# Second mixing of a fused attention kernel: eight chunks of 56 keys in place of four of 112

## The chip, the cores and the metric

The kernel runs on one core of a Trainium2 chip. The metric is device time in microseconds (us) from the first to the last instruction of one launch, with what lies around it; lower is better. Engines are called as the profile calls them: PE is TensorE (PEld its weight loads, which have rows of their own), DVE is VectorE, ACT is ScalarE, POOL is GpSimd, SP is SyncE, which issues the DMAs.

## The reference

Attention whose heads are mixed twice by small matrices, over the scores and over the probabilities, and behind it a feed-forward layer. Shapes: 4 batches, 12 heads, 448 queries and keys, head size 64; 768 and 2048 features in the feed-forward.

```
scores = scale * q @ k^T                       # per batch and head
scores = einsum('bhij,hg->bgij', scores, w_pre)     # first mixing
attn   = exp(scores - max) / (sum + 1e-9)
attn   = einsum('bhij,hg->bgij', attn, w_post)      # second mixing
x      = (attn @ v), heads side by side        # 1792 x 768
h      = x @ w_in
out    = (h * sigmoid(1.702 * h)) @ w_out
```

## The kernel before

**Steps.** The attention is cut into 180 steps, 45 for each batch, of 10 queries (8 in a batch's last one). The scores of a block of queries go to DRAM, and a step reads back a tile `r` whose partitions are (query, head) pairs: two halves of 5 queries x 12 heads = 60 partitions each, at partitions 0 and 64. `mix` and `mix_two` (the first mixing) multiply it by a small block matrix (`wa`, `wq`) into the PSUM tile `mx`; `mix_two` does two steps at once on four tiles of 64 rows x 64 columns of PE. `peak` (DVE), `expo` (ACT), `shifted` (POOL) and `inverse` (DVE) make the unnormalised probabilities `e` and the inverse sums; `weigh_mix` (POOL) makes `wr`, the second mixing's block matrix with the inverse sums in it.

**The second mixing.** `post` (line 368) is the step that the change touches. Its products have `e` as the stationary operand (what is loaded into PE: 60 rows x 112 keys) and `wr` as the moving one (60 rows x 60 columns), both float32. The result is the mixed probabilities, transposed: keys on partitions, (head, query) along the free dimension. There are 4 chunks of 112 keys and 2 row halves, so 8 products a step; the row halves run on two tiles of 64 rows x 128 columns and write to two PSUM banks of the tile `pp`, of which there is one. In the profile each float32 product stands as two weight loads and two streams, so a step has 16 of each on line 377. Then `keep_whole` (ACT, batches 0 and 1, float32) or `keep_upper` and `keep_lower` (ACT and DVE, batches 2 and 3, a float16 pair) copy `pp` into `p`, and after 12 steps `context` (lines 419 and 430) multiplies `p` with `v`, 112 keys on the partitions in each of four products.

**The feed-forward.** `hidden` (line 589) and `project` (line 628) run products of 128x128 float16 weights with 448 columns in groups of 6. They are laid between the steps as soon as a batch's `x` is ready, and go on alone after the last step. The feed-forward weights are fetched, split into float16 pairs and stored back to DRAM during the first steps (`conversion`).

**What sets the order.** A planner inside the kernel (`run_all`) puts every piece of work, with an estimated duration, on a queue of its engine and emits the instructions in that order; the engines then run their queues in order and wait on semaphores. Its table `MODE` groups the PE work by the shape of PE's tiles, and it adds 0.1 us where two neighbours differ:

```
MODE = {"qk": 1, "pp": 1, "mx": 2, "av": 3}
if MODE.get(last) != MODE.get(j["kind"]):
    occ, at = occ + 0.1, at + 0.1
```

For `post` it reckons with 0.44 us, in both kernels. Where it sees PE idle for 0.5 us or more ahead of a product, `fill` (line 287) puts float32 products of a constant with itself there, 128x128x128, on the PSUM bank that the product is about to write; they keep PE active and compute nothing that is used.

Of the kernel before, what the change touches and what calls it, by code (L numbers as in the profile page):

```python
# [10 lines left out]
F16 = mybir.dt.float16  # L11
# [8 lines left out]
B, H, S, D = 4, 12, 448, 64  # L20
# [13 lines left out]
HI = GI // 2  # L34
GAP = 64
NPAIR = H // 2
NR, CP = 4, S // 4
NCC = DM // 128
NS = 8
SW = DFF // NS  # L40
# [5 lines left out]
def attention_then_feed_forward(ctx, tc, q, k, v, w_pre, w_post, w_in, w_out, out):  # L46
    nc = tc.nc
    ctx.enter_context(tc.manual_schedule())

    def pool(name, bufs=1, **kw):  # L50
        return ctx.enter_context(tc.tile_pool(name=name, bufs=bufs, **kw))

    keep, stat, flow = pool("keep"), pool("stat", 4), pool("flow")
# [4 lines left out]
    st = {}  # L58
# [69 lines left out]


    THIRDS = 3  # L130
    SH = {"q": [128, NPAIR // THIRDS, S], "k": [128, NPAIR // THIRDS, S], "v": [CP, H // THIRDS, NR * D]}
    SRC = {"q": q, "k": k, "v": v}

    def load(name, b, i, use, tag="op"):

        t = st[name, b, i] = flow.tile(SH[name], F32, name=f"{name}{use}{i}_{b}", tag=tag, bufs=THIRDS)
        w = t.shape[1]
        nc.sync.dma_start(out=t, in_=SRC[name][b][:, i * w:(i + 1) * w])

    def load_whole(name, b, i):  # L140

        t = st[name, b, i] = flow.tile(SH[name], F32, name=f"{name}f{i}_{b}", tag=f"{name}p{i}")
        w = t.shape[1]
# [43 lines left out]
    def pair_of(name, b, i):  # L187

        key = (name + "p", b, i)
        if key not in st:  # L190
            if name == "v":
                st[key] = flow.tile([CP, 2, H // THIRDS, NR * D], F16, name=f"vp{i}_{b}", tag=f"vp{i}")
            else:
                st[key] = flow.tile([128, 2, NPAIR // THIRDS, S], F16, name=f"{name}p{i}_{b}", tag=f"{name}p{i}")
        t = st[name, b, i]
        src = t.rearrange("p a b -> p (a b)")
        u, l = (st[key][:, x].rearrange("p a b -> p (a b)") for x in range(2))
        return u, l, src, st["s" + name, b][:t.shape[0], 0:1]

    def upper_part(name, b, i, eng):  # L200
        u, _, src, s = pair_of(name, b, i)
        if eng == "A":
            nc.scalar.activation(u, src, AF.Copy, scale=s)
        elif eng == "D":
            nc.vector.tensor_scalar(u, src, s, 1.0, op0=ALU.mult, op1=ALU.mult)
        else:
            nc.gpsimd.tensor_scalar(u, src, s, 1.0, op0=ALU.mult, op1=ALU.mult)

    def lower_part(name, b, i, eng="D"):
        u, l, src, s = pair_of(name, b, i)  # L210
        nc.vector.scalar_tensor_tensor(l, src, s, u, op0=ALU.mult, op1=ALU.subtract)


    def chunk(b, c):
        i0 = c * CI
        return i0, min(CI, S - i0)
# [9 lines left out]
    def bank(name, tag="gen", bufs=NBK):  # L226
        return ps.tile([128, 512], F32, name=name, tag=tag, bufs=bufs)
# [43 lines left out]
    def rows_of(g):  # L271
        return g * GI, min(GI, S - g * GI)
# [14 lines left out]
    def fill(t):  # L287
        if gap[0] >= 0.5:
            for _ in range(int((gap[0] - 0.25) / 0.213)):
                nc.tensor.matmul(t[:, :128], ones, ones, start=True, stop=True)  # L290
        gap[0] = 0.0
# [76 lines left out]
    def post(i):  # L368
        n = rows_of(steps[i][1])[1] // 2
        w = n * H  # L370
        e, wr = row.pop(("e", i)), row.pop(("wr", i))
        pp = ps.tile([128, 2, 512], F32, name=f"pp_{i}", tag="pp", bufs=1)
        fill(pp[:, 0])
        for jc in range(NR):
            for a in range(2):
                rs = slice(a * GAP, a * GAP + w)
                nc.tensor.matmul(  # L377
                    pp[:CP, a, jc * w:(jc + 1) * w], e[rs, jc * CP:(jc + 1) * CP], wr[rs, :, :n],
                    start=True, stop=True,
                )  # L380
        row["pp", i] = pp[:CP, :, :NR * w].rearrange("p a (x i) -> p x a i", i=n)

    def mixed_to(i):
# [23 lines left out]
    def context(b, c, pr):  # L407
        i0, n = chunk(b, c)
        if pr % 3 == 0:
            av = bank(f"av_{b}_{c}_{pr}")  # L410
            fill(av)
            st["av"] = av[:, :3 * n].rearrange("p (a i) -> p a i", i=n)
        av = st["av"]
        w = H // THIRDS
        if not AV16[b]:
            for jc in range(NR):
                for d in range(2):
                    h = 2 * pr + d
                    nc.tensor.matmul(  # L419
                        av[d * D:(d + 1) * D, pr % 3, :],  # L420
                        st["v", b, h // w][:, h % w, jc * D:(jc + 1) * D],
                        st["p", b, c][:, jc, h, :n],
                        start=(jc == 0), stop=(jc == NR - 1),
                    )
            return av
        terms = [(jc, i, j) for jc in range(NR) for i, j in ((0, 0), (0, 1), (1, 0))]
        for t, (jc, i, j) in enumerate(terms):
            for d in range(2):
                h = 2 * pr + d
                nc.tensor.matmul(  # L430
                    av[d * D:(d + 1) * D, pr % 3, :],
                    st["vp", b, h // w][:, i, h % w, jc * D:(jc + 1) * D],
                    st["p", b, c][:, j, jc, h, :n],
                    start=(t == 0), stop=(t == len(terms) - 1),
                )
        return av
# [165 lines left out]
    def tanh(u, fc):  # L602
        th = st["th", u, fc] = flow.tile([128, S], F32, name=f"th_{u}_{fc}", tag="th", bufs=2)
        nc.scalar.activation(th, st["h", u, fc], AF.Tanh, scale=st["ct", u][:, 0:1])  # L604

    def gated(u, fc):
        th = st["th", u, fc]
        nc.vector.scalar_tensor_tensor(th, th, 1.0, st["h", u, fc], op0=ALU.add, op1=ALU.mult)  # L608
# [62 lines left out]
    USES = {"r": 15, "near": 10}  # L671
    MARGIN = {"in": 1.5, "w64": 1.5, "wt": 1.0}
    CROSS, SAME, LOOK = 0.12, 0.04, 0.1
    MODE = {"qk": 1, "pp": 1, "mx": 2, "av": 3}

    def add(eng, occ, f, after=(), due=0.0, lat=None, size=0.0, takes=(), kind="", bias=0.0, behind=None, moves=""):

        occ = occ if isinstance(occ, dict) else {e: occ for e in eng.split("/")}
        if lat is None:
            lat = {e: o + (0.2 if e == "PE" else 0.1) for e, o in occ.items()}  # L680
        lat = lat if isinstance(lat, dict) else {e: lat for e in occ}
        j = {"eng": tuple(occ), "occ": occ, "lat": lat, "f": f, "due": due, "size": size, "takes": list(takes),
             "kind": kind, "moves": moves, "bias": bias, "left": 0, "then": [], "next": [], "at": None, "from": 0.0}
        for a in after:
            if a is not None:
                a["then"].append(j)
                j["left"] += 1
        if behind is not None:
            behind["next"].append(j)
            j["left"] += 1  # L690
        for x in j["takes"]:
            x[1].append(j)
        if not j["left"]:
            waiting.append(j)
        return j
# [44 lines left out]
    def run_all():  # L740

        last = ""
        while waiting:
            picks = []
            for e in list(free) + ["-"]:
# [15 lines left out]
                if best:  # L761
                    t = min(x[0] for x in best) + LOOK
                    picks.append(min((x for x in best if x[0] <= t), key=lambda x: (x[2]["due"] - (2.0 if e == "PE" and last in MODE and x[2]["kind"] in MODE else 0.0), x[0]))[1:] + (e,))
            assert picks, [(j["eng"], j["due"], [x[0] for x in j["takes"]]) for j in waiting][:20]
# [4 lines left out]
            if e == "PE":  # L769
                if MODE.get(last) != MODE.get(j["kind"]):  # L770
                    occ, at = occ + 0.1, at + 0.1
# [364 lines left out]
    for i in range(N):  # L1136
        if i + AHEAD < N:
            b, g = steps[i + AHEAD]
            n = i + AHEAD
# [25 lines left out]
        b, g = steps[i]  # L1165
# [20 lines left out]
    for u in range(NU):  # L1186
        s, b = units[u]
# [6 lines left out]
        for fc in range(SF):  # L1194
# [12 lines left out]
            a = add("A", 0.53, lambda u=u, fc=fc: tanh(u, fc), [j, ct], due + 0.2, 0.64, takes=[("th", th)])  # L1207
            d = add("D", 0.54, lambda u=u, fc=fc: gated(u, fc), [a], due + 0.3, 0.62)
# [43 lines left out]
def _layout(inputs):  # L1252

    a = {n: np.asarray(inputs[n]) for n in _INS}
    for n in ("q", "k"):
        a[n] = a[n].reshape(B, NPAIR, 2, S, D).transpose(0, 2, 4, 1, 3).reshape(B, 128, NPAIR, S)
    a["v"] = a["v"].reshape(B, H, NR, CP, D).transpose(0, 3, 1, 2, 4).reshape(B, CP, H, NR * D)
    a["w_post_t"] = a["w_post"]
    w = a["moe_w_in"].reshape(NCC, 128, NS, SW).transpose(2, 1, 0, 3)
    a["moe_w_in"] = np.ascontiguousarray(w).reshape(NS, 128, WN)  # L1260
    w = a["moe_w_out"].reshape(NS, SF, 128, DM).transpose(0, 2, 1, 3)
    a["moe_w_out"] = np.ascontiguousarray(w).reshape(NS, 128, WN)
    return {n: np.ascontiguousarray(a[n]) for n in _INS}
# [20 lines left out]
```

## Time and profile before

| what | us |
|---|---|
| median of 3 runs | 929.02 (928.87 to 931.21) |
| the profiled execution | 927.6 |
| its span, first to last instruction | 925.9 |
| PE busy | 901.5 |
| ACT busy | 562.6 |
| DVE busy | 542.5 |
| mean granted TensorE clock | 0.996 of full speed |

The time of the profiled execution is 1.7 us more than its span, and 1.4 us less than the median. The first step's second mixing begins at 21.1 us and the last one's ends at about 781 us; what follows is feed-forward alone. In rows of matmuls and weight loads, `60*112` is the part of PE's array in use (rows x columns), and `60x60` is the operand (partitions x elements).

### The profile page before, as it was taken

The numbers are of one execution on the slowest core, as the hardware profiler recorded it, in microseconds if no ns is written. First come the engines' busy times: TensorE is split into PE (matmuls) and PEld (weight loads), VectorE is DVE, ScalarE is ACT, GpSimd is POOL, SyncE is SP. The second block draws the span as 40 slices with busy tenths as digits, with TensorE's granted clock in tenths as the row PEclk, the third lists the DMA queues.
The fourth block names the chain that finished last, engine by engine and source line by source line (L and its number), as shares of the span: only waits on it lengthen the run. The fifth ranks groups of instructions, "written<-read, shape, count | busy, mean of one in ns | idle before, by whom it ended". The sixth has DMA issues, their size and how long they took to land.

```text
span 925.9 us, 22628 instructions
## 1 busy us (share of the span) xinstructions
PE 901.5 (97%) x8708; PEld 548.3 (59%) x8708; DVE 542.5 (59%) x1254; ACT 562.6 (61%) x1280; POOL 264.6 (29%) x518
## 2 busy tenths in 40 slices
PE   8998998999999999989999999999999999999998
PEld 4676676556565665655656555555656555555554
DVE  4656665876768977975456755457544553333233
ACT  4867776887678697854576565555555453323442
POOL 1312332332223513351116322332123332203332
PEclk9999999999999999999999999999999999999999
DMA  6878888889878998776677585466544322344322
GB/s 218 279 234 264 268 292 267 301 297 286 301 250 284 293 319 273 254 242 212 208 249 225 159 263 164 142 206 214 174 142 125 126 95 69 123 142 137 137 70 93
DMA packets 68270, 194.42 MB, mean 210 GB/s; under 512 B 10419, under 2 KB 35123, under 8 KB 68163
## 3 DMA queue, kind: packets, MB, share of 16 engines
q1 hardware_dynamic: 68163, 192.98, 63.9%
q8 instruction: 69, 1.13, 0.5%
q14 instruction: 38, 0.31, 0.1%
HBM read 136.32 MB, written 54.04 MB: 206 GB/s over the span
## 4 chain that ended last, share of the span: by engine, by line
PE 89%; DVE 5%; ACT 2%; DMA 2%; issue 1%; POOL 0%; SPq 0%; ACTq 0%; DVEq 0%; POOLq 0%
PE h L589 23%; PE po L628 23%; PE pp L377 16%; PE mx L333 7%; PE av L419 4%; PE qk L239 3%; PE av L430 3%; PE pp L290 3%; PE qk L249 3%; PE mx L319 1%; DMA qf<-in_q_dram 1%; ACT p L396 1%; DVE w_f L518 1%; DVE nm L338 1%; DVE w_p L557 1%
## 5 line engine op out<-in xcount | busy, mean ns | idle before, releaser
L589 PE MATMUL h<-x,wt 128*128 128x448 f16 x1152 | 244.2, 353 | 0.0
L628 PE MATMUL po<-g,wt 128*128 128x448 f16 x1152 | 241.4, 353 | 0.1
L377 PEld LDWEIGHTS pp<-wr,e 60*112 60x112 f32 (+1 forms) x2880 | 158.3, 175 | 62.9 <-issue 40.0
L377 PE MATMUL pp<-wr,e 60*112 60x60 f32 (+1 forms) x2880 | 177.8, 262 | 0.0
L628 PEld LDWEIGHTS <-wt 128*128 128x128 f16 x1152 | 108.9, 98 | 113.6 <-issue 17.9
L589 PEld LDWEIGHTS <-wt 128*128 128x128 f16 x1152 | 108.4, 98 | 103.5 <-issue 6.6
L656 POOL TENSOR_TENSOR acc<-acc,pt 128x448 f32<-128x448 f32 x83 | 99.6, 1201 | 149.6 <-ACT pt L650 141.4
L355 POOL TENSOR_SCALAR rs<-sm 124x1 f32<-124x1 f32 x180 | 44.5, 247 | 328.0 <-ACT e L345 325.4
L345 ACT ACTIVATE e<-mx,nm 124x448 f32<-124x448 f32 x180 | 114.6, 637 | 20.9 <-DVE nm L338 20.0
L338 DVE TENSOR_REDUCE nm<-mx 124x1 f32<-124x448 f32 x180 | 107.7, 616 | 26.8 <-PE mx L333 20.0
L608 DVE SCALAR_TENSOR_TENSOR th<-th,h 128x448 f32<-128x448 f32 x64 | 39.6, 619 | 137.1 <-ACT th L604 136.9
L650 ACT ACTIVATE pt<-po,ct 128x448 f32<-128x448 f32 x83 | 52.4, 633 | 84.4 <-PE po L628 81.6
L404 DVE TENSOR_TENSOR p<-pp,p 112x480 f16<-112x480 f32 (+1 forms) x90 | 58.7, 652 | 70.9 <-ACT p L400 70.8
L400 ACT CAST p<-pp 112x480 f16<-112x480 f32 (+1 forms) x90 | 50.5, 562 | 72.0 <-PE pp L377 71.5
L333 PE MATMUL mx<-r,wq 60*64 60x448 f32 (+1 forms) x672 | 84.5, 562 | 0.0
L396 ACT COPY p<-pp 112x480 f32<-112x480 f32 (+1 forms) x90 | 51.1, 567 | 40.1 <-PE pp L377 39.3
L604 ACT ACTIVATE th<-h,ct 128x448 f32<-128x448 f32 x64 | 40.5, 633 | 55.5 <-PE h L589 55.2
L652 DVE SCALAR_TENSOR_TENSOR acc<-po,ct,acc 128x448 f32<-128x448 f32 x85 | 57.6, 680 | 23.4 <-PE po L628 23.2
L260 ACT COPY sc<-qk 112x448 f32<-112x448 f32 (+1 forms) x124 | 61.8, 539 | 13.9 <-PE qk L249 9.2
L614 ACT ACTIVATE g<-th,gs 128x448 f16<-128x448 f32 x64 | 42.8, 668 | 24.3 <-DVE th L608 23.8
L508 POOL TENSOR_SCALAR w_f<-w_f 128x512 f32<-128x512 f32 x48 | 32.1, 670 | 74.3 <-ACT w_f L504 73.3
L366 POOL TENSOR_SCALAR wr<-wp,rs 124x60 f32<-124x60 f32 (+1 forms) x90 | 38.9, 433 | 48.6 <-DVE rs L360 34.7
(137 smaller groups left out, 1018.3 us busy)
## 6 DMA issues: line engine op xcount, KB each, us to landing
wt<-wd SPq DMA_DIRECT2D x64, 768.0 KB
r<-sd SPq DMA_DIRECT2D x317, 105.0 KB
sd<-sc SPq DMA_DIRECT2D x84, 392.0 KB
w<-in_moe_w_in_dram SPq DMA_DIRECT2D x24, 512.0 KB
w<-in_moe_w_out_dram SPq DMA_DIRECT2D x24, 512.0 KB
wd<-w_p SPq DMA_DIRECT2D x16, 768.0 KB
out_dram<-acc SPq DMA_DIRECT2D x24, 224.0 KB
kf<-in_k_dram SPq DMA_DIRECT2D x6, 448.0 KB
```

Of the source, the lines that this page charges most:

```text
L260: (nc.scalar.copy if eng == "A" else nc.vector.tensor_copy)(t[:n, x, :], two[x][:n, :S])
L333: nc.tensor.matmul(out, w[rs], r[rs], start=True, stop=True)
L338: nc.vector.tensor_reduce(nm[:K], row["mx", i][:K, :S], axis=AX.X, op=ALU.max, negate=True)
L345: nc.scalar.activation(e[:K], row.pop(("mx", i))[:K, :S], AF.Exp, bias=row.pop(("nm", i))[:K, 0:1], accum_out=sm[:K, 0:1],)
L377: nc.tensor.matmul(pp[:CP, a, jc * w:(jc + 1) * w], e[rs, jc * CP:(jc + 1) * CP], wr[rs, :, :n], start=True, stop=True,)
L396: nc.scalar.copy(mixed_to(i), row.pop(("pp", i)))
L404: nc.vector.tensor_tensor(p[1], row.pop(("pp", i)), p[0], op=ALU.subtract)
L589: nc.tensor.matmul(h, w[:, i, c, fc * 128:(fc + 1) * 128], x[:, j, c, :], start=(n == 0), stop=(n == len(terms) - 1),)
L628: nc.tensor.matmul(po, w[:, j, fc, e * 128:(e + 1) * 128], g[:, i, fc, :], start=(n == 0), stop=(n == len(terms) - 1),)
L650: nc.scalar.activation(pt, po, AF.Copy, scale=c)
L652: nc.vector.scalar_tensor_tensor(a, po, c, a, op0=ALU.mult, op1=ALU.add)
L656: nc.gpsimd.tensor_tensor(a, a, st.pop(("pt", u, e)), op=ALU.add)
```

## The change

The keys of a step are cut into 8 chunks of 56 instead of 4 of 112. Two neighbouring chunks go to PSUM partitions 0 to 63 and 64 to 119 of `pp`, so that with the two row halves there are four tiles of 64 rows x 64 columns, and 16 products a step. The lower chunk of a pair loads 64 columns of `e`, its own 56 and 8 of the next chunk, so that all of partitions 0 to 63 are written. `v` is laid out to match by the host: 128 partitions with rows of zeros at 56 to 63 and 120 to 127, so that the 8 extra keys add nothing; `context` then multiplies over 120 partitions instead of 112. In the planner's table the second mixing takes the mode of `mx`.

```diff
-NR, CP = 4, S // 4
+NR, CJ = 4, S // 8
+CP = 64 + CJ
...
-    SH = {"q": [128, NPAIR // THIRDS, S], "k": [128, NPAIR // THIRDS, S], "v": [CP, H // THIRDS, NR * D]}
+    SH = {"q": [128, NPAIR // THIRDS, S], "k": [128, NPAIR // THIRDS, S], "v": [128, H // THIRDS, NR * D]}
...
         for jc in range(NR):
-            for a in range(2):
-                rs = slice(a * GAP, a * GAP + w)
-                nc.tensor.matmul(
-                    pp[:CP, a, jc * w:(jc + 1) * w], e[rs, jc * CP:(jc + 1) * CP], wr[rs, :, :n],
-                    start=True, stop=True,
-                )
+            for d in range(2):
+                j0, m = (2 * jc + d) * CJ, CJ if d else GAP
+                for a in range(2):
+                    rs = slice(a * GAP, a * GAP + w)
+                    nc.tensor.matmul(
+                        pp[d * GAP:d * GAP + m, a, jc * w:(jc + 1) * w], e[rs, j0:j0 + m], wr[rs, :, :n],
+                        start=True, stop=True,
+                    )
...
-                        st["v", b, h // w][:, h % w, jc * D:(jc + 1) * D],
+                        st["v", b, h // w][:CP, h % w, jc * D:(jc + 1) * D],
...
-    MODE = {"qk": 1, "pp": 1, "mx": 2, "av": 3}
+    MODE = {"qk": 1, "pp": 2, "mx": 2, "av": 3}
```

The new mode makes the planner order PE's queue anew. In all, PE's queue has 2880 products on `pp` in place of 1440, 143 filling products in place of 176, and 448 places where the tile shape changes in place of 463.

On PE, in the third batch's steps 98 to 100, the queue of before is this (`pp_..<-ones` and `h_..<-ones` are filling products, `pp_..<-wr` is the second mixing, `mx` the first, `sums` a small sum for the weights' conversion, `h` the feed-forward):

```order
L290 MATMUL pp_5721<-ones 128x128 x13
L377 MATMUL pp_5721<-wr_5626,e_5566 112x60 x8
L123 MATMUL sums_5749<-w_7_m,ones 128x3
L333 MATMUL mx_5751<-r_5641,wq_4054 64x448 x2
L333 MATMUL mx_5752<-r_5678,wq_4054 64x448 x2
L290 MATMUL pp_5792<-ones 128x128 x8
L377 MATMUL pp_5792<-wr_5717,e_5638 112x60 x8
L333 MATMUL mx_5813<-r_5694,wq_4054 64x448 x2
L333 MATMUL mx_5814<-r_5704,wq_4054 64x448 x2
L290 MATMUL h_0_5840<-ones 128x128 x10
```

The queue of the change at its step 99 is this:

```order
L124 MATMUL sums_6479<-w_7_m,ones 128x3
L334 MATMUL mx_6481<-r_6268,wq_4719 64x448 x2
L334 MATMUL mx_6482<-r_6286,wq_4719 64x448 x2
L380 MATMUL pp_6495<-wr_6393,e_6342 64x60 x2
L380 MATMUL pp_6495<-wr_6393,e_6342 56x60 x2
L380 MATMUL pp_6495<-wr_6393,e_6342 64x60 x2
L380 MATMUL pp_6495<-wr_6393,e_6342 56x60 x2
L380 MATMUL pp_6495<-wr_6393,e_6342 64x60 x2
L380 MATMUL pp_6495<-wr_6393,e_6342 56x60 x2
L380 MATMUL pp_6495<-wr_6393,e_6342 64x60 x2
L380 MATMUL pp_6495<-wr_6393,e_6342 56x60 x2
L334 MATMUL mx_6525<-r_6407,wq_4719 64x448 x2
```

The 8 products of a step have become 16, in four groups of four, each group on four different tiles; they stand between products of `mx` on tiles of the same shape, and the 31 filling products that stood here are gone. Over the steps 93 to 103 before had 36 filling products and the change has 3; over the steps 55 to 70 it is the other way about, 6 before and 24 now.

## Rows read from the trace of the kernel before

**Rows 1.** The chain that ended last: share of the span by engine, by line.

```profile
PE 89%; DVE 5%; ACT 2%; DMA 2%; issue 1%; POOL 0%; SPq 0%; ACTq 0%; DVEq 0%; POOLq 0%
PE h L589 23%; PE po L628 23%; PE pp L377 16%; PE mx L333 7%; PE av L419 4%; PE qk L239 3%; PE av L430 3%; PE pp L290 3%; PE qk L249 3%; PE mx L319 1%; DMA qf<-in_q_dram 1%; ACT p L396 1%; DVE w_f L518 1%; DVE nm L338 1%; DVE w_p L557 1%
```

**Rows 2.** Busy us (count): PE, PEld, DVE, ACT, POOL; then clock, DMA share, GB/s.

```profile
21.00:440.00 419.00, 401.50 (x4089) 262.50 (x4090) 300.62 (x725) 306.26 (x735) 129.75 (x274) 0.99 0.84 273
440.00:781.00 341.00, 340.61 (x3676) 201.75 (x3674) 186.51 (x409) 195.71 (x444) 92.98 (x192) 1.00 0.55 174
```

**Rows 3.** Line 377's streams: us, busy us (count), clock, DMA share, GB/s.

```profile
21.00:380.00 359.00, 91.39 (x1486) 0.99 0.86 281
380.00:440.00 60.00, 11.09 (x182) 1.00 0.70 229
440.00:782.00 342.00, 75.28 (x1216) 1.00 0.55 173
```

**Rows 4.** PE's longest wait: line, waited for, us in total, times, longest.

```profile
PE pp L290 <- ACT p L396: 9.4, 13, 1.6
```

**Rows 5.** PE in order of time: start, us, line, operation, count.

```profile
315.20 1.00 PE L377 MATMUL pp<-wr,e 60*112 60x60 f32 x16
316.04 0.73 PE L249 MATMUL qk<-kp,qp 64*112 64x448 f16 x6
...
776.98 1.00 PE L377 MATMUL pp<-wr,e 60*112 60x60 f32 x16
777.91 1.31 PE L589 MATMUL h<-x,wt 128*128 128x448 f16 x6
...
780.28 0.99 PE L377 MATMUL pp<-wr,e 48*112 48x48 f32 x16
781.20 1.31 PE L628 MATMUL po<-g,wt 128*128 128x448 f16 x6
```

**Rows 6.** Weight loads of one `pp`, three short windows, each counting loads under way.

```profile
301.08 0.18 PEld L377 LDWEIGHTS pp<-wr,e 60*112 60x112 f32 x2 [0.37 <-issue]
301.17 0.28 PEld L377 LDWEIGHTS pp<-wr,e 60*112 60x112 f32 x4
301.66 0.28 PEld L377 LDWEIGHTS pp<-wr,e 60*112 60x112 f32 x4
```

**Rows 7.** Duration of loads, ns min/median/max, by line.

```profile
L377 PEld LDWEIGHTS pp<-wr,e x2880: 169/175/308, 21.1 to 781.0; 60*112 60x112 f32 x188, 48*112 48x112 f32 x4
L333 PEld LDWEIGHTS mx<-r,wq x672: 129/130/133, 56.8 to 769.3; 60*64 60x64 f32 x164, 48*64 48x64 f32 x4
```

**Rows 8.** One `mx` on four tiles: windows 140.22 to 140.26, loads also to 140.31.

```profile
140.23 0.15 PEld L333 LDWEIGHTS mx<-r,wq 60*64 60x64 f32 x4
140.23 0.21 PEld L333 LDWEIGHTS mx<-r,wq 60*64 60x64 f32 x8
140.23 0.61 PE L333 MATMUL mx<-r,wq 60*64 60x448 f32 x4
```

**Rows 9.** PE in order of time: products with `v`.

```profile
98.40 2.68 PE L419 MATMUL av<-p,vf 112*64 112x120 f32 x48
101.01 0.39 PE L123 MATMUL sums<-w_m,ones 128*128 128x3 f32 x2
...
790.38 1.60 PE L430 MATMUL av<-p,vp 112*64 112x88 f16 x72
791.92 1.31 PE L589 MATMUL h<-x,wt 128*128 128x448 f16 x6
```

**Rows 10.** PE in order of time where filling products stand.

```profile
401.73 3.17 PE L290 MATMUL pp<-ones 128*128 128x128 f32 x26 [1.65 <-DVE p L404]
404.83 1.00 PE L377 MATMUL pp<-wr,e 60*112 60x60 f32 x16
```

**Rows 11.** Busy time by stretch: 21 to 380 us, and 10 us of it.

```profile
21.00:380.00 359.00, 345.90 (x3615) 227.77 (x3616) 257.08 (x629) 272.99 (x662) 110.40 (x244) 0.99 0.86 281
...
240.00:250.00 10.00, 10.00 (x75) 5.66 (x74) 5.98 (x14) 5.43 (x12) 4.25 (x7) 1.00 0.99 355
```

More of the change, by code (lines that the diff above doesn't have):

```diff
@@ L191, in pair_of @@
             if name == "v":
-                st[key] = flow.tile([CP, 2, H // THIRDS, NR * D], F16, name=f"vp{i}_{b}", tag=f"vp{i}")
+                st[key] = flow.tile([128, 2, H // THIRDS, NR * D], F16, name=f"vp{i}_{b}", tag=f"vp{i}")
             else:
@@ L431, in context @@
                     av[d * D:(d + 1) * D, pr % 3, :],
-                    st["vp", b, h // w][:, i, h % w, jc * D:(jc + 1) * D],
+                    st["vp", b, h // w][:CP, i, h % w, jc * D:(jc + 1) * D],
                     st["p", b, c][:, j, jc, h, :n],
@@ L1256, in _layout @@
         a[n] = a[n].reshape(B, NPAIR, 2, S, D).transpose(0, 2, 4, 1, 3).reshape(B, 128, NPAIR, S)
-    a["v"] = a["v"].reshape(B, H, NR, CP, D).transpose(0, 3, 1, 2, 4).reshape(B, CP, H, NR * D)
+    v = np.zeros((B, 2, 64, H, NR, D), a["v"].dtype)
+    v[:, :, :CJ] = a["v"].reshape(B, H, NR, 2, CJ, D).transpose(0, 3, 4, 1, 2, 5)
+    a["v"] = v.reshape(B, 128, H, NR * D)
     a["w_post_t"] = a["w_post"]
```

## The prediction

> **What bounds the kernel now.** I read the chain of work that ended last first: 89% of it is PE, and line 377, the second mixing, is 16% of the span, behind the two lines of the feed-forward with 23% each [rows 1]. The busy times by stretch say where that holds. From 440 to 781 us PE is busy for 340.6 of 341 us, while ACT is at 196 and DVE at 187: there a microsecond less on PE is a microsecond less in the end. From 21 to 440 us PE is busy for 401.5 of 419 us, so 17.5 us are waits, and the DMA engines are at a share of 0.84 [rows 2]. Behind 781 us only feed-forward runs, which the change does not touch. The streams of line 377, 16 a step, divide the 180 steps: 93 lie between 21 and 380 us, 11 between 380 and 440, and 76 behind [rows 3]. PE's largest wait is that of filling products ahead of the second mixing, which wait for ACT's copy out of the one `pp` tile, 9.4 us in 13 places [rows 4].
>
> **One second mixing, before.** Where the next work uses tiles of the same shape (`qk`, 64x112) it begins 0.84 us after the mixing did; before a feed-forward product, on the whole array, it is 0.93 [rows 5]. So a change of tile shape costs 0.09 us and the mixing itself 0.84.
>
> What sets the 0.84 is the question on which everything rests. The weight loads come in pairs, one for each row half: the first pair at 301.08, the second at 301.17, the seventh at 301.66. That is 0.58 us for six rounds, 0.097 us each; eight rounds and a last stream of some 0.05 make 0.83 [rows 6]. In each round a tile does a load of 112 columns and a stream of 60. If load and stream lay one behind the other, both would count; if the load lies under the stream of the round before, only the longer counts. The last step of a batch tells which: its streams have 48 columns instead of 60, a fifth less, and it takes 0.92 us up to the next work against 0.93 [rows 5]. So the loads set the round, and the streams are hidden under them.
>
> **One second mixing, after.** It has 16 products, so 32 loads and 32 streams on four tiles: eight rounds again, but with loads of 64 or 56 columns.
>
> - The load: one of 64 columns lasts 130 ns in the profile, one of 112 columns 175 [rows 7]. That is 45 ns less, so a round goes from 0.097 to 0.052. The first mixing shows it directly on the same tile shape: four loads have begun by 140.26 and the next four, each behind the first of its own tile, by 140.31 [rows 8].
> - The stream: 24 rounds of 120 float32 columns take 2.61 us with a change of shape behind them, so about 0.105 each and 0.052 for 60 columns [rows 9]. It is now as long as the load; one hides the other.
> - Four tiles at once: in the first mixing four streams have started within 0.03 us of each other [rows 8], so a round of four starts fits into 0.054.
>
> I take 0.054 a round: 8 x 0.054 + 0.05 for the last stream + 0.02 for the stagger is 0.50 us, 0.34 less. The lower bound is 0.052 a round, 0.49 in all. The upper bound is the densest long run of products on two tiles in the trace, 72 in 1.54 us or 21 ns each [rows 9]: 32 x 0.021 + 0.05 is 0.73. I take the value near the lower bound, since the rows behind it are of the same tile shape and operand type, while the 21 ns are explained by the 88 columns that each pair streams there.
>
> A rule speaks against this. The Trainium skill (TensorE: Matmul & The Clock Gate, Back-to-back issue gap) puts any stream of 1 to 64 columns at about 60 cycles, a floor of some 25 ns from start to start; its page TensorEngine Tiling (Array Packing), Instruction Overhead, therefore advises against taking a tiling factor from a dimension that is already small. By that floor, an estimate from the first page, 32 streams would take 0.80 us and the mixing 0.85, as long as now. The four starts within 0.03 us in the first mixing do not agree with it across tiles.
>
> **The sum.** Full price, with PE as the only bound:
>
> - 180 steps x 0.34 = 61.2 us.
> - Filling products: 33 fewer. Thirteen of them take 3.10 us up to the mixing [rows 10], of which some 0.2 are the first load and the change of shape, so 0.22 each: 7.4 us. Nearly all lies in the steps 93 to 103, where 36 become 3; the 18 more in the steps 55 to 70 are made up by fewer elsewhere.
> - 15 fewer changes of tile shape x 0.09 = 1.4 us.
>
> That is 70 us. From 440 us on I take all of it: 76 x 0.34 = 25.8. From 21 to 440 us it would be 104 x 0.34 + 7.4 = 42.8, and there I take two thirds, 28.5. Two things take the rest. First the DMA engines: from 21 to 380 us they are busy for 0.86 x 359 = 309 us [rows 11], and that work stays (the 16 more rows of `v` add a seventh to its 18 loads alone). Without 93 x 0.34 = 32 us the stretch would be 327 us long and the share 0.94. Ten microseconds at 0.99 do occur with PE fully busy [rows 11], but nothing as long as this; at 0.92 the stretch takes 335 us, and 8 of the 32 us are lost. Second the copies out of `pp`: with the mixing shorter, the next step's products come to the one tile sooner, while ACT's and DVE's copies (120 partitions instead of 112, the same free size) take as long as before. Where these copies bound the step they still do; 6 us is my allowance for it, beside the 9.4 us that this wait comes to now [rows 4]. The context products contract over 120 rows instead of 112 and stream the same columns, so they cost nothing more; the additional rows of `v` cost DMA time alone, hidden by loads ahead of their use.
>
> So 28.5 + 25.8 + 1.4 = 55.7 us. The profiled execution takes 927.6 us; it becomes 872. The median of the runs shown lies 1.4 us above it, so I forecast 873.
>
> **The rivals.**
>
> - *Starts set the round* (partial gain). If streams can't start closer than the 21 ns, a mixing takes 0.73 and saves 0.11: 76 x 0.11 + 1.4 + two thirds of (104 x 0.11 + 7.4) = 22 us, 907. For it: no long run in the trace is denser. Against it: the four starts of [rows 8]. With the page's floor nothing is saved on the mixing, only fills and shapes, two thirds of 7.4 + 1.4, about 6 us: 923, still faster by more than 0.3%.
> - *The first 440 us give nothing*: DMAs, ACT and DVE hold the steps at their pace. Then 25.8 + 1.4 remain: 902. For it: the share of 0.86, and ACT at 273 of 359 us [rows 11]. Against it: PE waits for 17.5 us in these stretches [rows 2], and DMA is 2% of the chain [rows 1].
> - *Loads on the same rows go one behind the other* (slower). If the two column tiles over one row half share the path of their loads, a round has two loads, 0.108 us, and the mixing takes 8 x 0.108 + 0.05 + 0.02 = 0.93: 180 x 0.09 = 16 us more, less 8 for fills and shapes, so 937. It decides from a round of about 0.102 on, where the 8 us are used up. Against it: in [rows 8] four loads are followed by four more within 0.08 us of the first start; in pairs one behind the other the fourth second load would come only after some 0.15.
> - *The change does not do what it says*: the planner's new order brings waits that eat the gain, and the time stays within 0.3%. Nothing in the profile speaks for it, but it is a new order of some 180 steps.
>
> **How the numbers follow.** The forecast has 0.74 (own range 860 to 888: from nearly the full 70 us to a third given back beside what I allow). The starts have 0.07, the first 440 us without a gain 0.09, the slower case 0.05, no change 0.05. A difference of 0.3%, 2.8 us, is about what a measurement of this kernel can tell from no change. Faster is 0.74 + 0.07 + 0.09 = 0.90, the same 0.05, slower 0.05. The range for 8 in 10 goes from 858, where all 70 us come through, to 903, which takes in the second rival and leaves the others out.
>
> **What would show it.** Right: on the mixing's line, twice the loads at a duration of about 130 ns, four in each round, rounds of 0.052 to 0.056, and the next work of the same tile shape about 0.50 us after a mixing's start; the stretch behind 440 us shorter by about 26 us with PE still full; a DMA share above 0.9 before 380 us. Wrong: rounds of 0.085 and more (starts set them), or of 0.1 (loads in turn); or rounds as forecast, but PE's waits between 21 and 440 us grown from 17.5 to 45 us and more, on copies or on transfers. A granted clock that falls below the 0.99 of this stretch would also cost what I have not counted.

## The result and the profile after

The changed kernel takes 875.7 us (median of 4 runs, 872.83 to 878.93) against 928.94 (4 runs) for the kernel before on the same chip: a ratio of 0.9424, 95% interval 0.9387 to 0.9461. The forecast was 873, with a range of 858 to 903. The profiled execution, the fastest of the four, has a span of 871.1 us, 54.8 less than before.

The chain that ended last, by engine and by line, after the change; it answers to [rows 1]:

```profile
PE 77%; DVE 8%; DMA 6%; ACT 5%; issue 2%; SPq 1%; POOL 0%; ACTq 0%; DVEq 0%; POOLq 0%
PE po L631 23%; PE h L592 23%; PE pp L380 9%; PE mx L334 6%; PE av L433 3%; PE av L422 3%; PE qk L240 3%; PE qk L250 2%; DMA r<-sd 2%; PE pp L291 2%; DVE nm L339 1%; ACT e L346 1%; ACT waste L111 1%; DMA w<-in_moe_w_in_dram 1%; DMA w<-in_moe_w_out_dram 1%
```

The second mixing went from 16% of a longer span to 9% of a shorter one. PE gave up 12 points of the chain to all the others; DMA has 6% where it had 2%.

PE in order of time around three steps: start, us, line, operation, count; it answers to [rows 5].

```profile
502.34 0.98 PE L334 MATMUL mx<-r,wq 60*64 60x448 f32 x8
503.15 0.63 PE L380 MATMUL pp<-wr,e 60*64 60x60 f32 x32
503.71 1.34 PE L250 MATMUL qk<-kp,qp 64*112 64x448 f16 x12
...
507.09 0.68 PE L380 MATMUL pp<-wr,e 60*64 60x60 f32 x32
507.70 1.31 PE L592 MATMUL h<-x,wt 128*128 128x448 f16 x6
...
517.16 0.68 PE L380 MATMUL pp<-wr,e 60*64 60x60 f32 x32
517.64 0.96 PE L334 MATMUL mx<-r,wq 60*64 60x448 f32 x8
```

Where the next work has the same tile shape (`mx`) it begins 0.48 us after the mixing did, 517.16 to 517.64. Where the shape changes it is 0.61, 507.09 to 507.70, against 0.93 before. (The first mixing in the fence follows `mx`, on the same tile shape, and its first four loads begin at 502.77 us, under the last streams of that; so its 0.56 is a little short.)

Duration of its loads, ns min/median/max (all forms together; the end of the row counts some of them by form); it answers to [rows 7]:

```profile
L380 PEld LDWEIGHTS pp<-wr,e x5760: 122/129/228, 20.2 to 726.2; 60*56 60x56 f32 x101, 60*64 60x64 f32 x94, 48*64 48x64 f32 x3, 48*56 48x56 f32 x1
```

Busy time by stretch, up to the 105th second mixing and from there to the last: us, then PE, PEld, DVE, ACT, POOL, clock, DMA share, GB/s; it answers to [rows 2].

```profile
20.20:411.00 390.80, 372.96 (x5761) 227.52 (x5760) 301.15 (x723) 306.10 (x742) 125.96 (x273) 0.99 0.88 297
411.00:726.00 315.00, 311.44 (x4799) 173.29 (x4796) 185.64 (x407) 192.13 (x437) 87.24 (x186) 1.00 0.58 188
```

The kernel before reached its 105th mixing at 443.2 us, 422.1 after its first; the changed one needs 390.8. So the first 104 steps gave 31.3 us and the remaining ones, 337.1 against 314.8, gave 22.3. PE is no longer full in the second stretch: it stands for 3.6 us there where it stood for 0.4. In the first it stands for 17.8 us, as long as before (17.7). PE's largest waits (line, waited for, us, times, longest), to be read against [rows 4]:

```profile
PE pp L291 <- ACT p L399: 10.6, 11, 2.1
PE pp L380 <- ACT p L399: 2.0, 3, 0.9
```

Two reasons could be behind the 53 us: the tiles' smaller loads at work four at a time (my theory), or the new order of PE's queue; and what kept the gain from the full 70 us could be transfers, copies or the clock. The runs below separate them. Ratios are those to the kernel before on the same chip.

### The profile page after: what moved, and what is told of

Read it like the earlier page. It is cut to its first block, busy times and chain, and to the rows that moved or that the text cites. A ratio compares the mean times of both kernels' runs of the same rounds, so it can differ in the third digit from the quotient of the medians.

```text
span 871.1 us, 28255 instructions
## 1 busy us (share of the span) xinstructions
PE 843.6 (97%) x11522; PEld 485.0 (56%) x11522; DVE 542.8 (62%) x1251; ACT 559.4 (64%) x1282; POOL 255.2 (29%) x511
## 4 chain that ended last, share of the span: by engine, by line
PE 77%; DVE 8%; DMA 6%; ACT 5%; issue 2%; SPq 1%; POOL 0%; ACTq 0%; DVEq 0%; POOLq 0%
PE po L631 23%; PE h L592 23%; PE pp L380 9%; PE mx L334 6%; PE av L433 3%; PE av L422 3%; PE qk L240 3%; PE qk L250 2%; DMA r<-sd 2%; PE pp L291 2%; DVE nm L339 1%; ACT e L346 1%; ACT waste L111 1%; DMA w<-in_moe_w_in_dram 1%; DMA w<-in_moe_w_out_dram 1%
## 5 line engine op out<-in xcount | busy, mean ns | idle before, releaser
L380 PEld LDWEIGHTS pp<-wr,e 60*56 60x56 f32 (+2 forms) x5760 | 101.9, 131 | 67.7 <-issue 39.3
L659 POOL TENSOR_TENSOR acc<-acc,pt 128x448 f32<-128x448 f32 x75 | 86.0, 1147 | 139.8 <-ACT pt L653 130.0
L380 PE MATMUL pp<-wr,e 60*64 60x60 f32 (+2 forms) x5760 | 123.0, 221 | 3.5 <-ACT p L399 2.0
L334 PE MATMUL mx<-r,wq 60*64 60x448 f32 (+1 forms) x672 | 90.4, 549 | 1.4 <-ACT e L346 0.7
L653 ACT ACTIVATE pt<-po,ct 128x448 f32<-128x448 f32 x75 | 47.5, 634 | 68.5 <-PE po L631 66.4
L407 DVE TENSOR_TENSOR p<-pp,p 120x480 f16<-120x480 f32 (+1 forms) x90 | 58.5, 649 | 51.7 <-ACT p L403 51.6
L403 ACT CAST p<-pp 120x480 f16<-120x480 f32 (+1 forms) x90 | 50.5, 561 | 60.6 <-PE pp L380 60.3
L655 DVE SCALAR_TENSOR_TENSOR acc<-po,ct,acc 128x448 f32<-128x448 f32 x93 | 63.2, 679 | 23.4 <-PE po L631 22.7
L399 ACT COPY p<-pp 120x480 f32<-120x480 f32 (+1 forms) x90 | 51.6, 573 | 27.6 <-PE pp L380 27.4
L617 ACT ACTIVATE g<-th,gs 128x448 f16<-128x448 f32 x64 | 42.8, 668 | 22.9 <-DVE th L611 22.0
L621 DVE SCALAR_TENSOR_TENSOR g<-th,gs,g 128x448 f16<-128x448 f32 x64 | 45.6, 712 | 12.7 <-ACT g L617 9.6
```

The source lines that it names most:

```text
L334: nc.tensor.matmul(out, w[rs], r[rs], start=True, stop=True)
L380: nc.tensor.matmul(pp[d * GAP:d * GAP + m, a, jc * w:(jc + 1) * w], e[rs, j0:j0 + m], wr[rs, :, :n], start=True, stop=True,)
L399: nc.scalar.copy(mixed_to(i), row.pop(("pp", i)))
L403: nc.scalar.copy(p[0], row["pp", i])
L407: nc.vector.tensor_tensor(p[1], row.pop(("pp", i)), p[0], op=ALU.subtract)
L655: nc.vector.scalar_tensor_tensor(a, po, c, a, op0=ALU.mult, op1=ALU.add)
```

## The experiments

**Loads and streams by themselves (micro).** The kernel has only rows of products like these, in the profile's float32 form, one line for each pair of sizes (columns loaded, columns streamed, tiles used):

```diff
+    (112, 60, 2, a_112_60), (112, 12, 2, b_112_12), (112, 120, 2, c_112_120),
+    (64, 60, 4, d_64_60), (56, 60, 4, e_56_60), (64, 12, 4, f_64_12),
+    (40, 12, 4, g_40_12), (40, 4, 4, h_40_4)
```

> Leaves out the whole computation but rows of float32 products (60 rows contracted) of one size each, 128 of a kind, and writes zeros; only the spacing of the products in its trace counts. Loads and streams hide each other (the theory): a round of two tiles with loads of 112 columns takes about 0.097 us with streams of 60 and of 12 columns alike, and 0.105 with 120; a round of four tiles takes 0.057 with loads of 64 and streams of 60, 0.052 with 56 and 60, still 0.057 with 64 and 12, and 0.04 or less with loads of 40. Starts set the round (the rival, 21 to 25 ns for each stream): every round of four tiles takes 0.084 to 0.1 us, whatever its sizes. Load and stream one behind the other (a second rival): 112 and 12 takes 0.05 us less than 112 and 60.

Loads under way in eight windows of it: us, PEld busy (count of loads), granted clock, DMA share, GB/s. The windows lie, in this order, in the runs of 112/60, 112/12, once more 112/12, 112/120, 64/60, 56/60, 64/12 and 40/12.

```profile
18.00:28.00 10.00, 10.00 (x208) 1.00 0.03 11
34.50:39.50 5.00, 5.00 (x104) 1.00 0.01 3
40.00:53.00 13.00, 13.00 (x144) 0.50 0.00 1
60.00:70.00 10.00, 10.00 (x198) 1.00 0.01 3
78.00:81.00 3.00, 3.00 (x215) 1.00 0.03 5
88.00:90.00 2.00, 2.00 (x164) 1.00 0.04 8
98.00:100.00 2.00, 2.00 (x143) 1.00 0.03 8
110.70:112.70 2.00, 2.00 (x217) 1.00 0.03 8
```

A window also counts the few loads under way as it begins. The starts of the single loads give, at full clock, a round of 98 ns for 112/60 and 98 again for 112/12, 102.5 for 112/120, 58 for 64/60, 52.5 for 56/60, 58 for 64/12 and 38 for 40/12 and 40/4. A load of 112 columns hides streams of 12 and of 60 equally; a stream of 120 sets its own round. Every number fits the larger of load and stream, and the rivals fall: neither do the two add up, nor do starts set a round of four tiles. The floor of 25 ns from start to start, which the Trainium skill gives (TensorE: Matmul & The Clock Gate, Back-to-back issue gap), does not hold across tiles: four starts fit into 38 ns here, 9.5 each.

**Two column halves in turn (halves_in_turn).** The same sixteen products, but neighbours use two tiles only:

```diff
-        for jc in range(NR):
-            for d in range(2):
+        for d in range(2):
+            for jc in range(NR):
```

> The changed kernel with the two column halves one after the other: the eight products of partitions 0 to 63 first, then the eight of 64 to 119, so that neighbouring products use two tiles and not four. If the gain comes from four tiles working at once, a mixing has 16 rounds of 0.052 to 0.058 us, 0.93 to 0.98 in place of 0.48, and the time is 940 to 955 us, slower than before the change. If only the size of the loads or the mode in the planner's table matters, it stays within 3 us of 876.

It took 905.72 us, ratio 0.974 (0.9707 to 0.9774): 30 us slower than the change, so that tiles work side by side is worth most of it, but not the 65 us and more that I expected. PE in order of time in this kernel shows why:

```profile
507.19 0.92 PE L380 MATMUL pp<-wr,e 60*64 60x60 f32 x32
508.05 1.34 PE L250 MATMUL qk<-kp,qp 64*112 64x448 f16 x12
```

A mixing takes 0.86 us with a change of shape, not 1.05. In the single records of the mixing at 503.97 us, the second half's first stream starts 0.291 us after the first half's, whose last streams start at 0.454 and 0.460. The tiles do not run in turn: products of the second half overtake those of the first that wait for their own tile, from about five rounds in. The Trainium skill says that matmuls start and end in program order (TensorE: Matmul & The Clock Gate, Part 3: Packing small matmuls — row/col tiling); the starts of this run do not agree across tiles. My expectation had sixteen rounds in a row; the overlap makes it about thirteen.

**The order alone (plan_only)** and **the products alone (products_only).** The first is the kernel before with the new entry of the planner's table, the second the changed kernel with the old one.

```diff
-    MODE = {"qk": 1, "pp": 1, "mx": 2, "av": 3}
+    MODE = {"qk": 1, "pp": 2, "mx": 2, "av": 3}
```

> The kernel before with only the entry of the planner's table changed: the old eight products of 112 keys in the new order of PE's queue. If the products are the gain, the order alone is worth the 33 filling products fewer (7 us at most) and nothing for shapes: 920 to 929 us. If the new order is what gains, it comes to 880 to 900.

> The changed kernel with the old entry of the planner's table: the sixteen products in the old order, 176 filling products. If the products are the gain, 876 to 888 us: 61 us of shorter mixing less some 14 of waits, without the 7 us of filling products. If the new order is what gains, 910 to 925.

The order alone took 917.2 us, ratio 0.9871 (0.9844 to 0.9898); the products alone 885.64, ratio 0.9521 (0.9494 to 0.9548). So the products are worth 4.8%, some 45 us, and the order 1.3%, some 12; together 6.1%, beside 5.8% for both. The products alone lie in the range expected; the order alone lies below its range, for it gains 12 us where I had priced 7 at most. The spans between the mixings say where each lies. The table gives the us saved against the kernel before, in one profiled execution each, from the start of one mixing to that of another:

| steps | both | order alone | products alone |
|---|---|---|---|
| 0 to 12 | -0.3 | -4.4 | 0.7 |
| 12 to 40 | 11.3 | 6.5 | 5.1 |
| 40 to 82 | 3.4 | -2.9 | 8.6 |
| 82 to 104 | 16.9 | 14.4 | 2.1 |
| 104 to 179 | 22.3 | -2.8 | 23.8 |

Behind step 104 the products give 24 us and the order takes 3; ahead of it the products give 16.5 and the order 13.6. The largest part of that, 14.4, lies in the steps 82 to 104, where the 36 filling products stood ([rows 10] has 13 of them); the three stretches ahead of these nearly cancel.

Busy time up to the 105th mixing, columns as in [rows 2]: before, the order alone, the products alone.

```profile
21.00:443.20 422.20, 404.55 (x4169) 265.00 (x4168) 302.50 (x729) 308.38 (x739) 130.26 (x276) 0.99 0.84 274
21.20:429.80 408.60, 398.43 (x4099) 258.60 (x4098) 302.85 (x723) 308.43 (x742) 125.88 (x273) 0.99 0.86 282
20.50:426.20 405.70, 378.15 (x5833) 232.97 (x5833) 302.11 (x729) 307.03 (x739) 129.08 (x276) 0.99 0.86 287
```

PE stands for 17.7 us before, for 10.2 with the order alone and for 27.5 with the products alone. So the order gives fewer waits beside fewer filling products, and the products cost waits. Now the streams of the mixing in the same stretch, before and after the change, and then the filling products, before and after:

```profile
21.00:443.20 422.20, 102.48 (x1664) 0.99 0.84 274
20.20:411.00 390.80, 71.78 (x3328) 0.99 0.88 297
21.00:443.20 422.20, 51.11 (x346) 0.99 0.84 274
20.20:411.00 390.80, 42.82 (x280) 0.99 0.88 297
```

The mixings are 30.7 us shorter there and the filling products 8.3, together 39 us, while PE's busy time fell by 31.6 only. By these rows the rest of PE's work in the stretch took some 7 us longer.

**Loads of 56 everywhere (load56).** `pp` becomes one tile for all steps, set to zero once, and the lower chunks load their own 56 columns:

```diff
-                j0, m = (2 * jc + d) * CJ, CJ if d else GAP
+                j0, m = (2 * jc + d) * CJ, CJ
```

> The changed kernel with 56 columns loaded for the lower chunks too; `pp` is one tile for all steps, set to zero once at the start, so partitions 56 to 63 stay zero. If the lower tiles' loads of 64 columns set the length of a mixing (rounds of 0.058 us on them, 0.052 on the upper ones), all rounds become 0.052, a mixing is 0.04 us shorter, and 180 of them are worth up to 7 us: 869 to 873. If what sets the time by now are waits on copies or transfers, it stays at 876.

It took 869.86 us, as expected, ratio 0.9348 (0.9318 to 0.9378), against 0.9424 for the change; the two intervals do not meet. A mixing before a shape change takes 0.58 us (506.74 to 507.32), 0.03 less:

```profile
506.74 0.64 PE L380 MATMUL pp_all<-wr,e 60*56 60x60 f32 x32
507.32 1.31 PE L592 MATMUL h<-x,wt 128*128 128x448 f16 x6
```

So the 64-column loads of the lower tiles set the length of a mixing in the change, as `micro` says, and 8 columns less of them are worth 6 us by the medians (2.9 us between the two profiled executions). The edit changes one thing more, a single `pp` tile for all steps; but PE's waits, which this could have shortened, are not shorter: 20.4 us from 20 to 440 us, against 17.8 in the change.

**Transfers (more_dma, more_dma_before, less_dma, less_dma_before).** One pair adds a transfer behind each fetch of the feed-forward's weights, the other leaves two of three fetches out (their thirds of a weight slice are then the first third's, so the output is another one):

```diff
+            more = flow.tile([128, HW], I32, name=f"{nm}_more_{a}", tag="more", bufs=2)
+            nc.sync.dma_start(out=more, in_=src[:, a * HW:a * HW + HW // 2].bitcast(I32))
```

```diff
         def fetch(a):
+            if a:
+                t["w", a] = t["w", 0]
+                return
```

> The changed kernel with 48 more transfers of 256 KB (12.6 MB in all, into a tile that nothing reads), one behind each fetch of the feed-forward weights. At the 300 GB/s of that stretch they are some 40 us of work for the DMA engines. If transfers hold the first 440 us of the changed kernel, the time rises by 15 to 40 us, to 890 to 915. If the lost part is waits on copies and the planner's order, it rises by less than 6.

> The same 48 transfers in the kernel before, whose DMA engines have more room. If transfers are what gives back the gain, this one rises by less than half of what the changed kernel rises by: 930 to 940. If both rise by as much, or neither, the transfers are no reason for the difference between the two.

> The changed kernel with 32 of the 48 fetches of the feed-forward weights left out (the first third of each slice is used three times), 16.8 MB or some 55 us of the DMA engines' work in the first 440 us; the rest of the order is the same. If transfers hold the steps there, the time falls by 8 to 20 us, to 856 to 868. If copies and the order do, by less than 3.

> The same left out in the kernel before. If transfers take a larger share of the changed kernel's path than of this one's, it falls by clearly less than the changed kernel does: 0 to 6 us, to 923 to 929.

| | in the changed kernel | in the kernel before |
|---|---|---|
| 12.6 MB more | 890.13 us, 0.957 (0.9542 to 0.9597) | 936.71 us, 1.0062 (1.0033 to 1.0091) |
| as they are | 875.7 us, 0.9424 (0.9387 to 0.9461) | 1 |
| 16.8 MB less | 870.84 us, 0.9353 (0.9325 to 0.9382) | 928.59 us, 0.9985 (0.9963 to 1.0008) |

Three of the four lie in the ranges expected, `more_dma` at the very edge of its own; `less_dma` misses its 856 to 868. More transfers cost the changed kernel 14 us and the old one 6; fewer give the changed one 6 and the old one nothing that can be told. So transfers do take part of the gain; with 16.8 MB less, which brings the DMA share from 20 to 411 us down to 0.78, only some 6 us come back. The traces don't show where: this run reaches its 105th mixing 390.0 us after the first, the change 390.8. What the transfers that are left still take is not shown. Busy time of this kernel in that stretch:

```profile
20.00:411.00 391.00, 369.88 (x5794) 225.78 (x5792) 300.32 (x724) 307.03 (x744) 127.03 (x274) 0.99 0.78 255
```

And PE's largest wait in it:

```profile
PE pp L291 <- ACT p L399: 12.1, 11, 2.3
```

PE still stands for 21 of 391 us, no less than in the change, and its largest wait is still the one for the copy out of `pp`.

**Filling products (no_fill).** The loop of `fill` is left out of the changed kernel.

> The changed kernel without any filling product. If they only lengthen the path (they run behind the wait for the bank, and 143 of them take 32 us), the time falls by 10 to 30 us, to 846 to 866. If they stand where PE would wait for other inputs anyway, it stays within 3 us of 876. If they hold the granted clock up, half speed covers more than the 10 us of now, and the time rises.

It took 869.73 us, ratio 0.9356 (0.9325 to 0.9388): 6 us less, out of 32 us of filling products, between two of the cases that I had named. PE's busy time from 20 to 440 us and the granted clock there, first this run, then the change:

```profile
20.00:440.00 420.00, 378.86 (x5857) 216.17 (x5858) 314.95 (x751) 321.20 (x783) 130.04 (x284) 0.96 0.88 290
```

```profile
20.00:440.00 420.00, 402.17 (x6167) 243.32 (x6169) 317.62 (x759) 325.82 (x792) 129.13 (x286) 0.99 0.88 293
```

PE's idle time goes up from 18 to 41 us, and the granted clock falls from 0.99 to 0.96. (The profiled execution took 875.69 us, the slowest of the six; the gain itself is not in these rows.) Most filling products thus stand where PE would wait anyway, and part of what their absence brings goes to half speed.

**Two versions on top of load56.** One keeps about half of the filling products, one tells the planner 0.48 us for the second mixing.

```diff
-            for _ in range(int((gap[0] - 0.25) / 0.213)):
+            for _ in range(int((gap[0] - 0.25) / 0.426)):
```

```diff
-        p = add("PE", 0.44, lambda: post(i), [w, e, posts.get(i - 1)], i + 1, takes=[("pp", pp)], kind="pp")
+        p = add("PE", 0.48, lambda: post(i), [w, e, posts.get(i - 1)], i + 1, takes=[("pp", pp)], kind="pp")
```

> The kernel with loads of 56 columns everywhere and about half of the filling products (one for each 0.426 us of a planned gap instead of 0.213). If part of what filling products cost comes back while the other part still holds the clock, 862 to 868; if the clock falls as without any, 866 to 872.

> Loads of 56 columns everywhere, and the planner reckons with 0.48 us for the second mixing, as measured, instead of 0.44. If an order made with the truer number fits the chip better, 862 to 868; if the order matters only by chance, within 5 us of 870 to either side.

They took 869.37 us, ratio 0.9333 (0.9299 to 0.9367), and 872.98, ratio 0.937 (0.9337 to 0.9402). Each lies where its second case had it, and neither can be told from load56 alone. Of the steps that keep the result, the loads of 56 columns are the one whose interval lies clear of the change's own; that of no_fill, at the same time, just touches it (0.9388 and 0.9387).

## Why the prediction was right

- *What sets a mixing.* Right. The last step of a batch, with streams a fifth shorter and the same length, had said that loads set the 0.84 us, and micro shows it without the kernel: 98 ns a round with streams of 60 and of 12 columns.
- *A round of 0.054 on four tiles, 0.50 us a mixing, 0.34 saved.* Right in size: 0.48 where the shape stays, 0.61 against 0.93 where it changes. The detail was wrong: there are no common rounds. The lower tiles, with loads of 64, go at 58 ns and the upper ones, with loads of 56, at 52.5; the lower ones set the end.
- *Behind step 104 all of it, 25.8 us.* The products gave 24; the new order took 3 back there, about half of it in waits (1.4 us in plan_only, where PE had hardly any), the other half in score products `qk` that it laid behind step 104 (174 in place of 168). Together 22.3; that PE would stay full there was wrong by the 3.6 us above.
- *Ahead of it two thirds of 42.8, 28.5 us.* The sum came out, 31.3, but not its parts. The products gave 16.5 of their full 35.4 us, less than half and not two thirds; the order gave 13.6 where its full price was 7.4 for filling products and a part of the 1.4 for shapes. What was left out is that an order can shorten waits: the products alone raised PE's waits from 17.7 to 27.5 us, the order alone lowered them to 10.2. Two errors cancelled, and that this number came out is luck.
- *What takes the gain back there.* Transfers take a part: with 16.8 MB less some 6 us come back, beside 8 in the forecast, though the sign named for it, a DMA share above 0.9, did not come; it is 0.88. The copies out of `pp` are PE's largest wait in every run, as expected, but all waits on them together went only from 11.5 to 13.6 us ahead of step 104, and all of PE's waits from 17.7 to 17.8. So what is missing of the 42.8 us is not in PE's waits but in its busy time: the mixings and the filling products gave some 39, and the rest of PE's work took some 7 us longer. The clock has a small part in that, half speed (1.2 GHz) for 10.2 us after the start against 6.8 before. How transfers come into it, and what the remainder is, no run shows; none had faster copies or a second `pp` tile.
- *Behind the last mixing.* Not only feed-forward runs there, as the texts ahead say, but the last `context` too [rows 9]. Nothing hangs on it: from the start of the last mixing to the end it is 145.6 us before and 145.3 after.
- *The rivals.* Starts do not set the round (micro), loads on the same rows do not go one behind the other (micro, with four loads in 58 ns), the first 440 us did give something, and the new order brought a gain of its own and no loss (plan_only).

## What to carry to other kernels

When a group of small products repeats at a fixed distance, find out first which of load and stream sets it: a row where only one of the two is shorter decides it, and cutting the stationary operand into more, narrower pieces pays where loads set it and tiles are free. By micro's rows the gain ends where load and stream are equally long, so the size to aim at is the one where they meet: 56 columns against 60 float32 columns here, and not 64. A table that a planner reads is a change of its own; run it alone and the products alone, since a sum that comes out can hide two errors.

## What the runs showed of the hardware

- Products on different tiles overtake each other: in halves_in_turn the second half began 0.291 us after the first, which started its last streams at 0.46.
- Long rows of small products come to a stop. In micro, PE worked through 239 streams and 240 loads in some 3.7 us on four tiles and then stood for 1.27 us with nothing to wait for; with loads of 56 it did so after 199. PE in order of time there:

```profile
77.84 3.72 PE L81 MATMUL pp<-e 60*64 60x60 f32 x239
82.83 0.46 PE L81 MATMUL pp<-e 60*64 60x60 f32 x17 [1.27 <-issue]
...
87.88 2.84 PE L84 MATMUL pp<-e 60*56 60x60 f32 x199
92.39 0.96 PE L84 MATMUL pp<-e 60*56 60x60 f32 x57 [1.67 <-issue]
```

  What PE waits for there the rows do not show.
- In micro's run of 112/12 loads were under way throughout, and the granted clock still fell from 1.00 to 0.50, that is from 2.4 to 1.2 GHz (the second and third windows above); with the same loads and streams of 60 columns it is 1.00 (the first window).
